# An attention and two mixing layers on one core: float16 products for a second piece, an earlier conversion, and one load for two weights

## The chip, the cores and the metric

The kernel runs on one core of one Trainium2 chip. The metric is device time in microseconds (us), the median of the runs; lower is better. The engines are PE (TensorE, the matrix products), DVE (VectorE), ACT (ScalarE) and POOL (GpSimd); SP issues the DMAs. Each engine works through its own queue in order, and semaphores hold one back until another has finished.

## The reference, cut to what matters

Three layers follow each other, all in float32 (the weights of the last two arrive as float64):

```python
# attention: q, k, v are (2, 8, 768, 64); 4 sink keys, window of 128
scores = where(is_sink | in_window, scale * q @ k.T, -1e9)
a = exp(scores - max); a = a / (sum(a) + 1e-9)
x = (a @ v)                                   # heads joined: (2, 768, 512)
# first mixing layer, 512 -> 2048 -> 512
xn = (x - mean) / sqrt(var + 1e-6) * g_ln
x = x + maximum(xn @ w_ch1, 0) @ w_ch2
# second mixing layer
theta = x @ w_theta
u = x + w_tok_r @ (x * cos(theta)) + w_tok_i @ (x * sin(theta))   # over the 768 tokens
out = u + maximum(u @ w_ch, 0)
```

## The kernel before, in words

The tokens are cut into six pieces of 256 (three for each of the two batches), each of two tiles of 128. Attention goes piece by piece and head by head. A head's scores are made by PE in a PSUM bank, DVE adds the mask and finds the maximum (L394), ACT makes the exponentials (L397), and the weights are transposed so that PE can multiply them with v. For pieces 2 to 5 the weights are split into two float16 parts and transposed by a DMA (`send_w`). For pieces 0 and 1 (`TURNED = 2`) PE transposes them in float32 (`turn_w`, L443), one copy brings them from PSUM to SBUF (ACT at even heads, L449, DVE at odd ones, L447), and the product with v is a float32 one (`values`, L477) with v as it was loaded (`whole_v`). Piece 1 also needs the sink keys: `turn_sinks` transposes their 16 columns (L457), and DVE copies them (L458). All products with v go through one PSUM bank of their own after the first piece, and DVE empties it (L494) before the next head's product.

For pieces 2 to 5 v is split into float16 parts, a high and a low one (`split_v`: ACT L196, DVE L198; the sink tile L190 and L198), from one staging buffer `vr`. There are five buffers for tiles of v, split and whole ones alike.

The first mixing layer runs in units. A unit multiplies one of 16 chunks of w_ch1 (`first`, L649 for units 0 to 7 in float32, L670 afterwards from split parts) and of w_ch2 (`second`, L696), each 128x512. Piece 0 takes units 0 to 15, piece 1 units 8 to 23, piece 2 units 16 to 31, and so on: from unit 8 on two pieces share a unit. The attention of the later pieces is interleaved with the units; the order on PE is written out by hand (`run`), with due times such as `READY1` by which a piece's attention must be done.

The weights are float64 in memory. `load_w12` loads a chunk's two matrices, one after the other, and `load64` turns each into float32: a DMA of 512 KB into one of four staging buffers, DVE L555, ACT L556 and L558, DVE L559, in that dependence. Chunks 0 to 3 are converted in the attention of piece 0 (`PRE`); afterwards unit u asks for the chunks up to u + 2 (u + 3 from unit 7 on), by `AHEAD = (2, 3)`. The ACT operations of such a conversion are placed behind the relu of unit u on ACT's queue (`behind`). The staging buffers are two x tiles that are not used yet (of pieces 4 and 5) and two of their own. The order on ACT, DVE and SP is made by a planner from its own estimates of durations; work of pieces 0 and 1 is put ahead in it (`ahead`).

Of the kernel before, what the change touches and what calls it, by code (L numbers as in the profile page):

```python
# [21 lines left out]
NT = S // 128  # L22
# [27 lines left out]
READY2 = 13.0  # L50
RATE = 7.0
PRE = [10, 15, 20, 24]
AHEAD = (2, 3)
START = 2
EARLY = 38.0

# [13 lines left out]
class Net:  # L70
# [110 lines left out]
    def split_v(self, b, t):  # L181

        if (b, t) in self.v3:
            return
        nc, p = self.nc, self.att
        r = p["vr"].tile([128, DM], F32, tag="vr", name="vr")
        nc.sync.dma_start(out=r, in_=self.vt[b, t])
        if t == NT:
            o = p["v"].tile([128, DM], F16, tag="vk", name="vk", bufs=1)
            nc.scalar.activation(o, r, AF.Copy, scale=VSC)  # L190
            r, lo, hi = r[64:96], o[64:96], o[64:96]
            self.v3[b, t] = o
# [82 lines left out]
    def attn_fast(self, eng):  # L275

        steps = [(piece, h) for piece in range(NP) for h in range(H)]
        nc, p, qk, scored, turned, sent, late = self.nc, self.att, {}, [], [], [], []

        def load(j, eng=eng):  # L280
            if j < len(steps):
                piece, h = steps[j]
                if h % 2 == 0:
                    qk[piece, h] = qk[piece, h + 1] = self.split_qk(piece, h // 2, eng)

        def load_v(piece):
            if piece < NP:
                b, tiles = self.tiles(piece)
                if piece < TURNED:
                    for t in tiles:  # L290
                        self.whole_v(b, t)
                    return
                for t in ([tiles[0] - 1] if tiles[0] else []) + tiles + ([NT] if tiles[-1] >= 2 else []):
                    self.split_v(b, t)

        def ahead(piece):
            return self.tc.high_priority() if piece < TURNED else ExitStack()

        def turn():

            piece, h, pt, st = scored.pop(0)
            b, tiles = self.tiles(piece)
            with ahead(piece):
                blocks = self.turn_w(pt, tiles, h)
            sinks = []
            if tiles[0]:
                p["ws"].append(p["ws"].pop(0))
                sinks = [p["ws"][-1][0:NSK, i] for i in range(PIECE)]
                if not turned:

                    pool, tag = self.vbanks[self.vturn % len(self.vbanks)]
                    self.vturn += 1
                    with ahead(piece):
                        self.turn_sinks(pool.tile([128, 512], F32, tag=tag, name="pv"), pt, sinks)
            turned.append((piece, h, blocks, sinks, st, pt))

        def finish(head):

            piece, h, blocks, sinks, st = head[:5]
            b, tiles = self.tiles(piece)  # L320
            with ahead(piece):
                self.values(b, h, tiles, piece, blocks, sinks, st, turned[0] if turned and turned[0][3] else None)
                if h % (H // 2) == H // 2 - 1:
                    self.stats(piece, h // (H // 2))
            if h == V_RANGE:
                while late:
                    q, ts = self.tiles(late.pop())
                    for t in ts:
                        if (q, t) in self.v3:
                            with self.behind():  # L330
                                self.range_v(q, t)
            if h == H - 1:
                with ahead(piece):
                    self.norm(piece)
                late.append(piece)

        load(0, self.nc.vector)
        load_v(0)
        for j, (piece, h) in enumerate(steps):
            b, tiles = self.tiles(piece)  # L340
            if h == 0:
                self.x[piece] = self.xp.tile([128, PIECE, DM], F32, tag=f"x{piece}", name=f"x{piece}")
            load(j + 2)
            if h == (3 if piece else V_NEXT) and piece != TURNED - 1:
                load_v(piece + 1)
            pt, st = yield from self.softmax(h, tiles, qk[piece, h])
            if piece < TURNED:
                scored.append((piece, h, pt, st))
            else:
                sent.append((piece, h) + self.send_w(pt, tiles) + (st,))  # L350
            if piece < TURNED and h == H - 1:

                while scored:
                    turn()
                    yield
                    finish(turned.pop(0))
                    yield
                while turned:
                    finish(turned.pop(0))
                if piece == TURNED - 1:  # L360
                    load_v(piece + 1)
                yield
                continue
            if len(scored) > (TURN if piece < TURNED else 0):
                turn()
                yield

            if len(turned) > (1 if scored else 0):
                finish(turned.pop(0))
            elif len(sent) > LAG:  # L370
                finish(sent.pop(0))
        while sent:
            yield
            finish(sent.pop(0))
        for t in tiles:
            self.range_v(b, t)
        self.range_whole()

    def softmax(self, h, tiles, qk):

        nc, p = self.nc, self.att
        n = len(tiles)
# [2 lines left out]
        for i, t in enumerate(tiles):  # L385
# [10 lines left out]
                op1=ALU.min, accum_out=st[:, 0, i:i + 1]),  # L396
                nc.scalar.activation(e, e, AF.Exp, bias=st[:, 0, i:i + 1], scale=-1.0,  # L397
                                     accum_out=st[:, 1, i:i + 1])]
        self.inverse(st, PSC * VSC if qk[1] is not None else 1.0)
        return pt, st  # L400

    def send_w(self, pt, tiles):
# [30 lines left out]
    def turn_w(self, pt, tiles, h):  # L433
# [7 lines left out]
        for x, (i, t) in enumerate(keys):  # L441
            c0 = (t + 1 - tiles[i]) * KW
            nc.tensor.transpose(ps[:, x * 128:(x + 1) * 128], pt[:, i, c0:c0 + 128], self.ident)  # L443
        wt = self.att["wt"].tile([128, m, 128], F32, tag="wt", name="wt")
        ps = ps[:, 0:m * 128].rearrange("p (m k) -> p m k", k=128)
        if h % 2:
            nc.vector.tensor_copy(wt, ps)  # L447
        else:
# [3 lines left out]
    def turn_sinks(self, bank, pt, sinks):  # L452
# [2 lines left out]
        ps = bank[0:NSK, 256:512].rearrange("p (i k) -> p i k", k=128)  # L455
        for i in range(PIECE):
            nc.tensor.transpose(ps[:, i], pt[:, i, 128:128 + NSK], self.ident)  # L457
        nc.vector.tensor_copy(self.att["ws"][-1][0:NSK], ps)  # L458

    def values(self, b, h, tiles, piece, blocks, sinks, st, after):  # L460

# [3 lines left out]
        pv = pool.tile([128, 512], F32, tag=tag, name="pv")  # L465
        hc = slice(h * D, (h + 1) * D)
        for i in range(len(tiles)):
            if piece < TURNED:
                prods = [(a, self.whole[b, t][:, hc]) for (j, e, t), a in blocks.items() if j == i]
                if sinks:  # L470
                    prods.append((sinks[i], self.whole[b, 0][0:NSK, hc]))
            else:
                prods = [(a, v[:, hc]) for (j, e, t), a in blocks.items() if j == i for v in self.v3[b, t][:2 - e]]
                if sinks:
                    prods.append((sinks[i], self.v3[b, NT][:, hc]))
            for j, (a, m) in enumerate(prods):
                nc.tensor.matmul(pv[:, i * D:(i + 1) * D], a, m, start=j == 0, stop=j == len(prods) - 1)  # L477
# [20 lines left out]
    def attn_general(self, eng):  # L498

        nc, p = self.nc, self.att  # L500
        for piece in range(NP):
            b, tiles = self.tiles(piece)
            self.x[piece] = self.xp.tile([128, PIECE, DM], F32, tag=f"x{piece}", name=f"x{piece}")
            if tiles[0] == 0:
                for t in range(NT):
                    self.load_v(b, t)
# [35 lines left out]
            self.norm(piece)  # L542
            yield


    def load64(self, src, stage, dst, tag):

        nc = self.nc
        n = dst.shape[-1]
        raw = stage.tile([128, n, 2], I32, tag=tag, name="raw")  # L550
        nc.sync.dma_start(out=raw.rearrange("p n w -> p (n w)"), in_=src.bitcast(I32))
        hi, flat = raw[:, :, 1], raw.rearrange("p n w -> p (n w)")
        half = flat.bitcast(U16).rearrange("p (n w) -> p n w", w=4)
        parts = dst.bitcast(U16).rearrange("p (n w) -> p n w", w=2)
# [14 lines left out]
    def load_w12(self, f):  # L569
        if f in self.w12f:  # L570
            return
        self.w12f[f] = []
        for e in range(2):
            t = self.wraw.tile([128, DM], I32, tag="w", name="w12")
            self.rawp.append(self.rawp.pop(0))
            self.load64(self.w12[f, e], self.rawp[-1][0], t, self.rawp[-1][1])
            self.w12f[f].append(t.bitcast(F32))

    def stats(self, piece, half):

# [239 lines left out]
    def run(self, general):  # L820
# [7 lines left out]
        rp = lambda name, bufs=1: pool("right", name, bufs, side="right")  # L828
        self.x, self.w12f, self.v3, self.xnorm, self.h, self.acc, self.bn, self.relu, self.whole = ({} for _ in range(9))
        self.xp = pool("all", "x")  # L830
        self.wraw = pool("left", "wraw", 2 * NF)
        self.wsp = pool("left", "wsp", 3)
        self.xT = pool("left", "xT")
        self.ln = pool("left", "ln")
# [13 lines left out]
        else:  # L848
# [3 lines left out]
            for w in a["wbuf"]:  # L852
                nc.gpsimd.memset(w[:, 0:PIECE], 0.0)
            ws = rp("a_ws")
            a["ws"] = [ws.tile([128, PIECE, 128], F32, name=f"ws{i}") for i in range(2)]
            raw = rp("a_raw")
            attn = self.attn_fast
        self.rawp = [(self.xp, f"x{NP - 2 + i}") for i in range(2)] + ([] if general else [(raw, f"r{i}") for i in range(2)])

        sb, hb, vb = (self.ps_s, "s"), (self.ps_h, "h"), (self.ps_v, "pv")  # L860
        ab = [(self.ps_a, f"a{i}") for i in range(4)]
# [237 lines left out]
```

## Time and profile before

| | |
|---|---|
| median of 3 runs | 623.66 us (617.91 to 625.28) |
| the profiled execution | 617.65 us, of which the span from first to last instruction is 615.9 us |
| mean granted TensorE clock in it | 0.983 |
| PE busy | 584.7 us, 95% |
| PE weight loads | 479.8 us, 78% |
| DVE busy | 408.5 us, 66% |
| ACT busy | 334.0 us, 54% |

The attention of piece 0 ends near 35 us, unit 0 starts at 44.6 us, the attention of piece 1 ends near 100 us, and unit 8 starts at 117.5 us. Busy shares are means over all stages; the first stages have other limits than the rest. PE's busy time is partly modelled, as its instructions overlap.

### The profile page before, as it was taken

What the parts mean: (1) busy time and instruction counts of PE and PEld (TensorE: products, weight loads), DVE (VectorE), ACT (ScalarE), POOL (GpSimd) and SP (SyncE); (2) the same over time, 40 slices, a digit from 0 to 9 for tenths busy, and PEclk for the clock granted to TensorE, in tenths of its full rate; (3) what the DMA queues carried; (4) which work ended last, traced back from release to release, by engine and by line L of the source; (5) the groups of instructions that cost most, each with busy time, mean ns of one, the idle gap of its engine ahead of it and who ended that gap; (6) DMA issues with size and microseconds to landing.
All of it is one profiled execution on the core that took longest, in us unless ns stands there. A gap on an engine that the chain in (4) does not pass through costs nothing.

```text
span 615.9 us, 9332 instructions
## 1 busy us (share of the span) xinstructions
PE 584.7 (95%) x3473; PEld 479.8 (78%) x3473; DVE 408.5 (66%) x925; ACT 334.0 (54%) x732; POOL 60.1 (10%) x53
## 2 busy tenths in 40 slices
PE   5969998899999999999999899999999899999996
PEld 3756666577777777777788678888999789999996
DVE  4763465889867776976775643367798789754262
ACT  3834563998755656655556633346676656532020
POOL 1000000000000000000021200001343332300100
PEclk9999997899999999999999989999999999999998
DMA  7641442789722533433312310000232322010112
GB/s 274 215 159 44 160 156 86 251 209 222 130 54 49 117 82 71 96 69 60 78 54 101 103 51 2 0 1 1 102 104 104 103 69 70 1 35 34 36 36 74
DMA packets 55367, 56.41 MB, mean 92 GB/s; under 512 B 40080, under 2 KB 43152, under 8 KB 55312
## 3 DMA queue, kind: packets, MB, share of 16 engines
q1 hardware_dynamic: 55312, 55.72, 32.0%
q8 instruction: 29, 0.48, 0.3%
q14 instruction: 26, 0.21, 0.1%
HBM read 43.12 MB, written 3.15 MB: 75 GB/s over the span
## 4 chain that ended last, share of the span: by engine, by line
PE 69%; DVE 13%; DMA 7%; ACT 6%; issue 2%; POOL 1%; SPq 0%; ACTq 0%; POOLq 0%
PE acc L696 19%; PE h L670 18%; PE s L273 9%; PE m L781 5%; PE f L812 5%; PE pv L477 5%; PE h L649 3%; DVE st L559 2%; DMA raw<-wtok 2%; DMA raw<-w 2%; PE th L740 2%; PE wp L443 2%; ACT st L558 1%; ACT raw L556 1%; DVE st L555 1%
## 5 line engine op out<-in xcount | busy, mean ns | idle before, releaser
L638 DVE TENSOR_TENSOR wl<-w,wh 128x512 fp32r<-128x512 f32 x96 | 69.0, 723 | 53.4 <-ACT wh L637 26.7
L637 ACT ACTIVATE wh<-w 128x512 fp32r<-128x512 f32 x96 | 59.9, 628 | 77.5 <-PE acc L696 44.0
L670 PE MATMUL h<-xT,wh 128*128 128x512 f32 (+1 forms) x384 | 96.8, 388 | 2.4 <-DVE w L555 2.4
L670 PEld LDWEIGHTS h<-xT,wh 128*128 128x128 f32 x384 | 67.1, 191 | 18.2 <-ACT xT L625 2.6
L696 PE MATMUL acc<-wh,hh 128*128 128x512 f32 x176 | 73.2, 416 | 0.0
L397 ACT ACTIVATE p<-p,st 128x272 f32<-128x272 f32 (+1 forms) x96 | 47.4, 494 | 43.7 <-DVE st L394 43.3
L696 PE MATMUL acc<-wl,hh 128*128 128x512 f32 x176 | 69.6, 395 | 0.0
L696 PE MATMUL acc<-wh,hl 128*128 128x512 f32 x176 | 69.5, 395 | 0.0
L394 DVE CUSTOM_DVE_ANT_0 p<-s,mask 128x272 f32<-128x272 f32 (+1 forms) x96 | 39.3, 411 | 29.7 <-PE s L273 28.9
L670 PE MATMUL h<-xT,wl 128*128 128x512 f32 (+1 forms) x192 | 48.8, 376 | 0.0
L696 PEld LDWEIGHTS acc<-wh,hh 128*128 128x128 f32 x176 | 33.5, 190 | 9.4 <-issue 1.2
L556 ACT ACTIVATE raw<-raw 128x512 f32<-128x512 f32 (+1 forms) x52 | 37.0, 715 | 6.5 <-DVE st L555 6.4
L670 PEld LDWEIGHTS h<-xT,wl 128*128 128x128 f32 x192 | 35.0, 191 | 6.8
L477 PE MATMUL pv<-v,wt 128*128 128x64 f16 (+1 forms) x472 | 38.2, 228 | 1.9 <-DVE x L494 1.9
L696 PEld LDWEIGHTS acc<-wh,hl 128*128 128x128 f32 x176 | 33.5, 190 | 7.8 <-DVE hl L675 0.3
L696 PEld LDWEIGHTS acc<-wl,hh 128*128 128x128 f32 x176 | 33.4, 190 | 6.0 <-DVE wl L638 0.4
L767 POOL TENSOR_TENSOR x<-xh,xl 128x512 f32<-128x512 f32 x12 | 19.3, 1607 | 131.1 <-DVE r L761 131.1
L597 POOL TENSOR_TENSOR rs<-rs,mhalf 128x2 f32<-128x2 f32 x6 | 4.8, 805 | 266.9 <-ACT rs L596 266.9
L675 DVE SCALAR_TENSOR_TENSOR hl<-h,hh 128x512 fp32r<-128x512 f32 (+1 forms) x48 | 30.7, 639 | 0.2 <-ACT hh L674 0.2
L273 PE MATMUL s<-raw 64*128 64x272 f32 (+1 forms) x64 | 24.1, 520 | 6.9 <-DMA raw<-qk 6.4
L558 ACT ACTIVATE st<-raw 128x768 uint16<-128x768 uint16 (+1 forms) x20 | 19.4, 971 | 18.6 <-DMA raw<-wtok 7.2
L674 ACT ACTIVATE hh<-h 128x512 fp32r<-128x512 f32 (+1 forms) x48 | 26.5, 552 | 5.5 <-PE h L670 5.5
(287 smaller groups left out, 1442.3 us busy)
## 6 DMA issues: line engine op xcount, KB each, us to landing
raw<-w SPq DMA_DIRECT2D x32, 512.0 KB, 4.3
raw<-wtok SPq DMA_DIRECT2D x12, 768.0 KB, 4.2
raw<-qk SPq DMA_DIRECT2D x16, 336.0 KB, 3.0
vr<-vt SPq DMA_DIRECT2D x14, 256.0 KB, 3.0
out_dram<-o SPq DMA_DIRECT2D x24, 128.0 KB, 1.7
raw<-qk SPq DMA_DIRECT2D x8, 272.0 KB, 4.0
raw<-wth SPq DMA_DIRECT2D x4, 512.0 KB, 3.3
raw<-wch SPq DMA_DIRECT2D x4, 512.0 KB, 3.3
```

Source lines behind the costliest of these rows:

```text
L273: self.nc.tensor.matmul(ps, q[:, c], k[:, k0:k0 + kn], start=j == 0, stop=j == len(prods) - 1)
L394: self.newest = [nc.vector.tensor_tensor_reduce(out=e, in0=ps[:, c0:WIN], in1=self.mask[min(t, 2)], scale=-0.125, scalar=3e38, op0=ALU.add ...
L397: nc.scalar.activation(e, e, AF.Exp, bias=st[:, 0, i:i + 1], scale=-1.0, accum_out=st[:, 1, i:i + 1])]
L477: nc.tensor.matmul(pv[:, i * D:(i + 1) * D], a, m, start=j == 0, stop=j == len(prods) - 1)
L556: nc.scalar.activation(hi.bitcast(F32), hi.bitcast(F32), AF.Copy, scale=2.0 ** -112)
L637: nc.scalar.activation(hi, r, AF.Copy)
L638: nc.vector.tensor_tensor(out=lo, in0=r, in1=hi.bitcast(F32), op=ALU.subtract)
L670: nc.tensor.matmul(ps[:, 0:n], a[:, k * 128:(k + 1) * 128], x[:, k, c], start=m == 0, stop=m == 11)
L675: nc.vector.scalar_tensor_tensor(out=hl, in0=ps[:, 0:n], scalar=0.0, in1=hh.bitcast(F32), op0=ALU.max, op1=ALU.subtract)
L696: nc.tensor.matmul(ps, a[:, c], w, start=m == 0 and n == 0, stop=m == NF - 1 and n == len(prods) - 1)
L781: nc.tensor.matmul(ps, z[i][e][:, c * 128:(c + 1) * 128], w[:, t], start=s == 0 and m == 0 and c % 2 == 0, stop=s == NT - 1 and m == 5 and ...
L812: nc.tensor.matmul(ps, self.w_last[k][e][:, c * 128:(c + 1) * 128], u[k][f], start=m == 0, stop=m == 11)
```

## The change

Piece 1 multiplies with v in float16 parts. Its weights are still transposed by PE in float32, but are brought from PSUM as two float16 parts, the high one by ACT and the low one by DVE, for every head; the sinks likewise. A block's product is high with high, high with low, and low with high. For that, piece 1's tiles of v are split like those of pieces 2 to 5, tiles 1, 2, 3 and the sink tile, and a low part `vl` of the sinks is added; only piece 0 uses whole v. `load_v(2)` now comes at head 3 of piece 1 and not at its end. `AHEAD` becomes (4, 4). A chunk's two matrices are loaded by one DMA of 1 MB and converted in one set of operations 1024 wide; the staging buffers become two of twice the size, and the x tiles of pieces 4 and 5 become one tile, `last`.

```diff
-AHEAD = (2, 3)
+AHEAD = (4, 4)
@@ split_v @@
+            if b == 0:
+                self.vl = p["v"].tile([128, DM], F16, tag="vl", name="vl", bufs=1)
+                nc.vector.scalar_tensor_tensor(out=self.vl[0:32], in0=r[0:32], scalar=VSC, in1=o[0:32], op0=ALU.mult,
+                                               op1=ALU.subtract)
@@ attn_fast @@
-                if piece < TURNED:
+                if piece == 0:
...
-                blocks = self.turn_w(pt, tiles, h)
+                blocks = self.turn_w(pt, tiles, h if piece == 0 else None)
...
-            if h == (3 if piece else V_NEXT) and piece != TURNED - 1:
+            if h == (3 if piece else V_NEXT):
                 load_v(piece + 1)
...
-                if piece == TURNED - 1:
-                    load_v(piece + 1)
@@ turn_w @@
+        if h is None:
+            wt = self.att["wt"].tile([128, 2 * m, 128], F16, tag="wt", name="wt")
+            nc.scalar.activation(wt[:, 0:m], ps, AF.Copy, scale=PSC)
+            nc.vector.scalar_tensor_tensor(out=wt[:, m:], in0=ps, scalar=PSC, in1=wt[:, 0:m], op0=ALU.mult,
+                                           op1=ALU.subtract)
+            return {(i, e, t): wt[:, e * m + x] for e in range(2) for x, (i, t) in enumerate(keys)}
@@ turn_sinks @@
-        nc.vector.tensor_copy(self.att["ws"][-1][0:NSK], ps)
+        ws = self.att["ws"][-1]
+        nc.scalar.activation(ws[0:NSK, 0], ps, AF.Copy, scale=PSC)
+        nc.vector.scalar_tensor_tensor(out=ws[0:NSK, 1], in0=ps, scalar=PSC, in1=ws[0:NSK, 0], op0=ALU.mult,
+                                       op1=ALU.subtract)
@@ values @@
+                if sinks and piece < TURNED:
+                    prods += [(sinks[i][e], v[0:NSK, hc]) for e, v in (
+                        (0, self.v3[b, NT]), (0, self.vl), (1, self.v3[b, NT]))]
@@ load_w12 @@
-        for e in range(2):
-            t = self.wraw.tile([128, DM], I32, tag="w", name="w12")
-            self.rawp.append(self.rawp.pop(0))
-            self.load64(self.w12[f, e], self.rawp[-1][0], t, self.rawp[-1][1])
-            self.w12f[f].append(t.bitcast(F32))
+        t = self.wraw.tile([128, 2 * DM], I32, tag="w", name="w12")
+        self.rawp.append(self.rawp.pop(0))
+        self.load64(self.w12[f].rearrange("e p n -> p e n"), self.rawp[-1][0], t, self.rawp[-1][1], 2)
+        t = t.bitcast(F32)
+        self.w12f[f] = [t[:, 0:DM], t[:, DM:]]
@@ run @@
-        self.rawp = [(self.xp, f"x{NP - 2 + i}") for i in range(2)] + ([] if general else [(raw, f"r{i}") for i in range(2)])
+        self.rawp = [(self.xp, "last")] + ([] if general else [(raw, "r")])
```

## Rows read from the trace of the kernel before

**Rows 1.** The head of the profile's page: the span.
```profile
span 615.9 us, 9332 instructions
```

**Rows 2.** Busy time by stretch: length, each engine's busy us, granted clock, DMA share, GB/s.
```profile
10.00:35.00 25.00, 25.00 (x95) 19.85 (x94) 17.40 (x62) 19.38 (x57) 0.00 (x0) 1.00 0.75 263
35.00:45.00 10.00, 5.04 (x16) 3.54 (x16) 7.05 (x21) 2.13 (x7) 0.71 (x1) 1.00 0.39 141
45.00:55.00 10.00, 10.00 (x34) 6.61 (x33) 1.79 (x7) 2.64 (x8) 0.00 (x0) 1.00 0.10 34
55.00:90.00 35.00, 34.28 (x173) 24.08 (x172) 19.16 (x61) 21.92 (x55) 0.00 (x0) 1.00 0.43 140
90.00:105.00 15.00, 12.99 (x46) 9.15 (x46) 7.30 (x18) 2.60 (x8) 0.83 (x1) 0.77 0.26 88
105.00:117.50 12.50, 10.14 (x46) 6.49 (x45) 11.33 (x31) 12.50 (x29) 0.00 (x0) 0.98 0.62 212
117.50:125.00 7.50, 7.48 (x20) 5.10 (x21) 6.60 (x18) 7.50 (x22) 0.00 (x0) 0.58 0.82 229
```

**Rows 3.** The chain that ended last, 55 to 131 us: start, duration, what.
```profile
55.11 1.92 PE h L649 x8
57.47 1.70 PE pv L477 x12
...
91.15 4.14 DMA raw<-w
...
96.40 3.24 PE pv L477 x12
99.64 3.71 PE h L649 x8
...
117.53 2.07 PE h L670 x4
...
120.57 3.57 PE h L670 x8
...
126.41 2.04 PE h L670 x8
128.44 0.42 PE pv L477 x14
```

**Rows 4.** Timeline of PE and ACT, 96 to 118 us: idle before, and its releaser, in brackets.
```profile
96.40 0.96 PE L477 MATMUL pv<-v,wt 128*128 128x64 f32 x4 [1.89 <-DVE x L494]
96.98 0.63 ACT L196 ACTIVATE v<-vr 128x512 f16<-128x512 f32 x1 [6.81 <-PE pv L477]
...
116.90 0.57 ACT L625 ACTIVATE xT<-tp 128x512 fp32r<-128x512 f32 x1
117.52 2.07 PE L670 MATMUL h<-xT,wh 128*128 128x512 f32 x4 [2.39 <-DVE w L555]
```

**Rows 5.** Groups by shape, 44.6 to 117.5 us: busy, mean ns; idle before.
```profile
L558 ACT ACTIVATE w<-raw 128x512 uint16<-128x512 uint16 x14 | 10.8, 770 | 0.0
L559 DVE SCALAR_TENSOR_TENSOR w<-raw,w 128x512 int32<-128x512 int32 x13 | 8.8, 680 | 2.4 <-ACT w L558 2.4
L556 ACT ACTIVATE raw<-raw 128x512 f32<-128x512 f32 x13 | 8.5, 655 | 0.0
L555 DVE TENSOR_SCALAR w<-raw 128x512 uint16<-128x512 uint16 x12 | 5.5, 457 | 9.0 <-DMA raw<-w 9.0
L458 DVE COPY ws<-pv 16x256 f32<-16x256 f32 x8 | 3.3, 410 | 6.9 <-PE pv L457 6.8
L447 DVE COPY wt<-wp 128x512 f32<-128x512 f32 x4 | 2.7, 679 | 0.9 <-PE wp L443 0.8
L449 ACT ACTIVATE wt<-wp 128x512 f32<-128x512 f32 x4 | 2.4, 588 | 2.1 <-PE wp L443 2.1
L198 DVE SCALAR_TENSOR_TENSOR v<-vr,v 128x512 f16<-128x512 f32 x2 | 1.4, 688 | 1.4 <-ACT v L196 1.4
L657 ACT ACTIVATE xT<-x 128x1024 fp32r<-128x1024 f32 x1 | 1.0, 1029 | 0.0
```

More of the change, by code (lines that the diff above doesn't have):

```diff
@@ L307, in turn @@
                 p["ws"].append(p["ws"].pop(0))
-                sinks = [p["ws"][-1][0:NSK, i] for i in range(PIECE)]
+                sinks = [[p["ws"][-1][0:NSK, e, i] for e in range(2)] for i in range(PIECE)]
                 if not turned:
@@ L341, in attn_fast @@
             if h == 0:
-                self.x[piece] = self.xp.tile([128, PIECE, DM], F32, tag=f"x{piece}", name=f"x{piece}")
+                self.x[piece] = self.new_x(piece)
             load(j + 2)
-            if h == (3 if piece else V_NEXT) and piece != TURNED - 1:
+            if h == (3 if piece else V_NEXT):
                 load_v(piece + 1)
-            pt, st = yield from self.softmax(h, tiles, qk[piece, h])
+            pt, st = yield from self.softmax(b, h, tiles, qk[piece, h])
             if piece < TURNED:
@@ L377, in attn_fast, with softmax @@
         self.range_whole()
-    def softmax(self, h, tiles, qk):
+    def softmax(self, b, h, tiles, qk):
         nc, p = self.nc, self.att
@@ L398, in softmax @@
                                      accum_out=st[:, 1, i:i + 1])]
-        self.inverse(st, PSC * VSC if qk[1] is not None else 1.0)
+        self.inverse(st, PSC * VSC if tiles[0] or b else 1.0)
         return pt, st
@@ L443, in turn_w @@
             nc.tensor.transpose(ps[:, x * 128:(x + 1) * 128], pt[:, i, c0:c0 + 128], self.ident)
+        ps = ps[:, 0:m * 128].rearrange("p (m k) -> p m k", k=128)
+        if h is None:
[4 more added lines that the diff above has]
+            return {(i, e, t): wt[:, e * m + x] for e in range(2) for x, (i, t) in enumerate(keys)}
         wt = self.att["wt"].tile([128, m, 128], F32, tag="wt", name="wt")
-        ps = ps[:, 0:m * 128].rearrange("p (m k) -> p m k", k=128)
         if h % 2:
@@ L467, in values @@
         for i in range(len(tiles)):
-            if piece < TURNED:
+            if piece == 0:
                 prods = [(a, self.whole[b, t][:, hc]) for (j, e, t), a in blocks.items() if j == i]
-                if sinks:
-                    prods.append((sinks[i], self.whole[b, 0][0:NSK, hc]))
             else:
                 prods = [(a, v[:, hc]) for (j, e, t), a in blocks.items() if j == i for v in self.v3[b, t][:2 - e]]
-                if sinks:
+                if sinks and piece < TURNED:
+                    prods += [(sinks[i][e], v[0:NSK, hc]) for e, v in (
+                        (0, self.v3[b, NT]), (0, self.vl), (1, self.v3[b, NT]))]
+                elif sinks:
                     prods.append((sinks[i], self.v3[b, NT][:, hc]))
@@ L502, in attn_general @@
             b, tiles = self.tiles(piece)
-            self.x[piece] = self.xp.tile([128, PIECE, DM], F32, tag=f"x{piece}", name=f"x{piece}")
+            self.x[piece] = self.new_x(piece)
             if tiles[0] == 0:
@@ L543, in attn_general, with new_x, load64 @@
             yield
-    def load64(self, src, stage, dst, tag):
+    def new_x(self, piece):
+        if piece < NP - 2:
+            return self.xp.tile([128, PIECE, DM], F32, tag=f"x{piece}", name=f"x{piece}")
+        if piece == NP - 2:
+            self.last = self.xp.tile([128, 2, PIECE, DM], F32, tag="last", name="last")
+        return self.last[:, piece - NP + 2]
+    def load64(self, src, stage, dst, tag, parts=1):
         nc = self.nc
@@ L550, in load64 @@
         raw = stage.tile([128, n, 2], I32, tag=tag, name="raw")
-        nc.sync.dma_start(out=raw.rearrange("p n w -> p (n w)"), in_=src.bitcast(I32))
+        flat = raw.rearrange("p n w -> p (n w)")
+        nc.sync.dma_start(out=flat if parts == 1 else flat.rearrange("p (e n) -> p e n", e=parts), in_=src.bitcast(I32))
         hi, flat = raw[:, :, 1], raw.rearrange("p n w -> p (n w)")
@@ L571, in load_w12 @@
             return
-        self.w12f[f] = []
-        for e in range(2):
-            t = self.wraw.tile([128, DM], I32, tag="w", name="w12")
-            self.rawp.append(self.rawp.pop(0))
-            self.load64(self.w12[f, e], self.rawp[-1][0], t, self.rawp[-1][1])
-            self.w12f[f].append(t.bitcast(F32))
+        t = self.wraw.tile([128, 2 * DM], I32, tag="w", name="w12")
[3 more added lines that the diff above has]
+        self.w12f[f] = [t[:, 0:DM], t[:, DM:]]
     def stats(self, piece, half):
@@ L830, in run @@
         self.xp = pool("all", "x")
-        self.wraw = pool("left", "wraw", 2 * NF)
+        self.wraw = pool("left", "wraw", NF)
         self.wsp = pool("left", "wsp", 3)
@@ L854, in run @@
             ws = rp("a_ws")
-            a["ws"] = [ws.tile([128, PIECE, 128], F32, name=f"ws{i}") for i in range(2)]
+            a["ws"] = [ws.tile([128, 2, PIECE, 128], F16, name=f"ws{i}") for i in range(2)]
             raw = rp("a_raw")
             attn = self.attn_fast
-        self.rawp = [(self.xp, f"x{NP - 2 + i}") for i in range(2)] + ([] if general else [(raw, f"r{i}") for i in range(2)])
+        self.rawp = [(self.xp, "last")] + ([] if general else [(raw, "r")])
         sb, hb, vb = (self.ps_s, "s"), (self.ps_h, "h"), (self.ps_v, "pv")
```

## The prediction

> **What bounds the kernel now.** The profiled execution took 617.65 us for a span of 615.9 us [rows 1]; the median of the three runs is 623.66 us, 6.0 us above it. I make the sum against 617.65 and subtract it from the median; that these 6 us stay is a choice.
>
> I read the stretches first, because the change acts only before some 160 us. In the view by stretch [rows 2] the reader is to see four states. From 10 to 35 us PE is busy throughout, with ACT 19.38 and DVE 17.40 of 25 us. From 35 to 45 us PE has half its time idle, in the norm of piece 0. From 45 to 90 us PE is all but full, while DVE and ACT are at about half. Then 90 to 125 us is bad: idle PE, a granted clock of 0.77 and later 0.58, ACT nearly empty until 105 us and full after it.
>
> The chain of waits [rows 3] says what fills PE there: a head's product with v is 12 matmuls in 1.70 us, about as long as a unit's whole first product (1.92). It also shows a weight DMA (4.14 us, landing at 95.29) standing ahead of a product. The timeline [rows 4] shows the two stalls. At 96.40 PE has waited 1.89 us for DVE's L494, and ACT stood 6.81 us at L196: the split of a tile of v found no free buffer until a product of piece 1 had read its whole tile. At 117.52 PE has waited 2.39 us before unit 8. The row names L555, but ACT's L625, one of this product's inputs, ended at 117.47: ACT's backlog is as good a releaser.
>
> **The product in float16.** A head has four blocks and two sink products, so 6 x 3 = 18 float16 matmuls replace its 12. Fourteen such matmuls of piece 2 take 0.42 us [rows 3], 0.030 each, so 18 take 0.54. That saves 1.70 - 0.54 = 1.16 us a head, and 8 x 1.16 = 9.3 us of PE.
>
> The price lies on the other two engines [rows 5]. Instead of one copy by either engine, ACT now makes a high part for each head and DVE a low part: ACT 4 more at 0.588, 2.4 us; DVE 4 more at 0.679, 2.7 us. For the sinks ACT gets 8 operations; no row shows that shape on ACT, so between 0.2 (below the DVE copy) and 0.588 each, and I take the DVE copy's 0.410, 3.3 us. DVE's subtraction replaces its copy at about the same price. The path from transposes to product becomes ACT then DVE. Its cover is the head between; if that is gone, the next thing late is the single PSUM bank, which L494 and both sink parts have to release.
>
> Does the PE gain survive? From 45 to 117.5 us DVE is busy 1.79 + 19.16 + 7.30 + 11.33 = 39.6 us and waits 9.0 us for weight DMAs [rows 2, 5]. Add 2.7 and one more chunk converted in this stretch, 2 x (0.457 + 0.680) = 2.3, and DVE needs 53.6 us, its waits included. PE would need 72.5 - 9.3 = 63.2, and some 56 if the stalls below went too. ACT comes to 39.7 + 2.4 + 3.3 + a chunk's 2 x (0.770 + 0.655) = 2.9, in all 48.3, less what wide operations save. So DVE becomes almost as long as PE. In-order queues don't run that full: the bounds are 0 and 9.3 us, and I take 6.3, nearer the upper end because PE still has the longer list.
>
> **The wider conversion.** One operation 1024 wide for two of 512: L657 is 1024 wide at 1.029 us, against 2 x 0.63 for L196 [rows 4, 5], 0.23 saved, by two operations and some seven chunks 3 us of ACT. That work is beside PE, so I count 0. The new cost is that DVE's first step waits for the whole 1 MB, and the next chunk's DMA on SP until all of a chunk is converted, with the q and k loads behind it in SP's queue. The pair of loads in the bad stretch landed 4.14 us after its release [rows 3], so one load of the same bytes should not be worse by more than another 4.14. I keep half of the 9.0 us of DVE waits, as the count halves.
>
> The Trainium skill ("DMA: Bandwidth & Descriptors", "Anatomy of one DMA") gives a fixed part of about 2.0 us and bytes over 436 GB/s, an estimate of 4.4 us for 1 MB. By it the waits would be no longer than now, and the sum some 1 us better; no row here shows a load of 1 MB.
>
> **Four units ahead.** Unit 0 now asks for chunk 4 and unit 1 for chunk 5, when ACT has 7.4 of 10 us free and DVE 8.2 from 45 to 55 us [rows 2]. Chunk 8, whose lateness shows at 117.52, is asked for by unit 4 and no longer by unit 6. Unit 7 asks for one chunk, no longer for two. So ACT's full stretch starts with less queued. What goes: 2.39 us of idle, and the low clock behind it, 2.07 - 1.02 and 3.57 - 2.04 (the full-clock row has 2.04 for eight) [rows 3, 4], 2.6 us; together 5.0. Norm and transposes of piece 1 remain before unit 8, so I take 4.2; bounds 0 and 5.0.
>
> **Splits of v.** Tiles 1, 2 and the sinks are split earlier, tile 4 and 5 find buffers that piece 0 has freed, and ACT's 6.81 us go. With them may go the first stall: 1.89 us of idle and the low clock behind it, 3.24 - 1.70 and 3.71 - 1.92, 3.3 us, of which 1.5 are in the product itself: 5.2 in all. But DVE's wait for a weight DMA was there too and may fall elsewhere; bounds 0 and 5.2, and I take half, 2.6. In return three splits and the low sinks fall mostly into 10 to 35 us: ACT 3 x 0.63 = 1.9 us and DVE 4 x 0.688 = 2.8 us, against 5.6 and 7.6 us free [rows 2]. One staging buffer serves them, so ACT can stand behind a landing, ahead of an exponential; piece 0 then ends later. Bounds -0.5 (two L555 of 0.457 among the norm's operations become one) and 3; I take 1.5. On SP two whole-tile loads go and three staged ones come, and the range check later loads one tile, not three: all beside other work, 0. The shared x tile costs 0, since the last chunk is asked for by unit 11 and piece 4 joins at unit 32.
>
> **Sum.** -6.3 - 4.2 - 2.6 + 1.5 = -11.6: 606.0 us for a profiled execution, 612 us beside the median. Nothing later changes except by starting earlier. Two per cent of 623.66 is 12.5 us, about what a measurement here can tell from no change, so the forecast lies just on the near side of that line.
>
> **Rivals.**
>
> *All of it* (chance 0.25). PE stays the only bound: 9.3 + 5.0 + (5.2 - the 1.5 counted in the product's own change at most) = 18 to 19.5 us; 604 to 606. For it: ACT's empty stretch from 90 to 105 us [rows 2] is filled. Against: DVE's 53.6 us of need.
>
> *Eaten by DVE and ACT* (0.22). Each head waits for the low part behind a weight DMA on DVE; or the lead is only nominal, because two staging buffers hold two chunks and the planner puts L555 right at a landing as before. Then the product brings 0 to 2, the stalls 2 to 4, and piece 0 costs 1.5: 0.5 to 4.5 us gained, 619 to 623.
>
> *PE's clock* (0.08), the slower side. The clock fell after the idle stretches before 96.40 and 117.52, and rows at the low level took 1.9 times as long (3.71 against 1.92) [rows 3]. If the shorter products leave PE waiting in each head from 45 to 105 us, the remaining 46 us or so of PE work run partly at 1.2 GHz. Each us of it costs 0.9; the 11.6 are gone after 13 us, and after 27 us it is slower by over 2%. With half of the 46 us low it is 21 - 11.6 = 9 us slower, 633; with all, 653. Against: from 35 to 45 us PE idled 5 us and the granted clock stayed at 1.00 [rows 2].
>
> The Trainium skill ("TensorE: Matmul & The Clock Gate", Part 1) makes the half rate the default that activity must lift, and so speaks against a change that thins PE's work. By that rule, this last rival would be the forecast wherever DVE leaves gaps; the trace agrees at 96 and 117 us and not at 35 to 45.
>
> **The numbers.** My own case has 0.45; its own range is 608 to 616, around 612, half a chance on either side of the 2% line at 611.2 shifted towards no change. Faster by over 2%: 0.25 + 0.19 = 0.44. Slower by over 2%: 0.06 of the clock case. Within: 0.50. The range for 8 in 10 reaches from 602, which takes in the whole gain, to 622, which takes in most of the eaten one.
>
> **What would show it.** Product: rows of 18 float16 matmuls near 0.54 us a head, and head to head some 0.8 us shorter; if that stays away, DVE or ACT bounds, and the idle before L477 will name which. Stalls: no ACT wait at L196, ACT busy in 45 to 55 us and spread in 90 to 125, granted clock 1.00 there, under 0.5 us of wait before unit 8. Waits for weight DMAs: half as many, under 5 us in all. Price: unit 0 starts at 46 us, against 44.6. I would be wrong if piece 0 ended over 3 us later, if a slice before 110 us showed a granted clock under 0.9, or if PE gained time before 120 us and lost it again by 160.

## The result, and the profile after

| | before | after |
|---|---|---|
| median | 624.27 us (617.91 to 625.28, 4 runs) | 613.65 us (612.30 to 616.41, 4 runs) |
| ratio | | 0.9896, interval [0.9853, 0.9939] |
| profiled execution | 617.65 us, clock 0.983 | 614.24 us, clock 0.985 |

The change makes the kernel 1.0% faster by the ratio, 6.5 us, and by 3.8 to 9.2 us over its interval; the two medians of four runs lie 10.6 us apart. The same kernel run again later gave 0.9881, 7.4 us (further down). The two profiled executions lie only 3.4 us apart, because the one of before is among its fastest: 6.6 us under this median, while that of after is 0.6 us above its own. A comparison of the two traces therefore shows only part of what the runs show.

Busy time by stretch, after; columns as in [rows 2] (length, then PE, PE's weight loads, DVE, ACT and POOL, granted clock, DMA share, GB/s):

```profile
35.00:45.00 10.00, 5.73 (x20) 4.52 (x20) 8.13 (x21) 3.46 (x11) 1.27 (x1) 1.00 0.70 257
45.00:55.00 10.00, 9.12 (x33) 6.71 (x32) 2.95 (x6) 4.96 (x8) 0.00 (x0) 1.00 0.07 26
...
90.00:105.00 15.00, 10.29 (x64) 6.47 (x65) 8.94 (x20) 6.96 (x15) 0.00 (x0) 0.69 0.30 104
105.00:117.50 12.50, 12.07 (x49) 7.17 (x48) 9.13 (x22) 11.38 (x26) 0.90 (x1) 0.96 0.42 127
117.50:125.00 7.50, 6.80 (x30) 4.63 (x30) 6.74 (x21) 6.65 (x17) 0.00 (x0) 1.00 1.19 222
```

Against [rows 2]: the granted clock of 117.5 to 125 us rose from 0.58 to 1.00, but that of 90 to 105 us fell from 0.77 to 0.69, and PE is busy 10.29 us there, no longer 12.99. One bad stretch is repaired, and PE stands idle longer in another. The deeper fall of the clock does not belong to the kernel: a second execution of it (the run with no edit among the experiments) has the same 10.29 us of PE there, but the clock of before, 0.77:

```profile
90.00:105.00 15.00, 10.29 (x57) 6.34 (x57) 9.44 (x20) 6.60 (x16) 0.00 (x0) 0.77 0.33 112
```

ACT works 4.96 us from 45 to 55 us, not 2.64: the lead does start the conversions there.

The chain of after through the bad stretch, and below it the timeline of the same place (idle before and its releaser in brackets):

```profile
85.58 3.62 PE h L671 x8
...
89.23 0.38 ACT hh L673
89.61 1.02 ACT raw L578
90.64 0.50 ACT p L400 x2
91.14 1.24 ACT w L580
...
92.41 0.97 DVE w L581
...
95.41 3.41 PE acc L718 x4
98.82 1.02 PE pv L490 x18
```

```profile
83.15 0.35 PE L490 MATMUL pv<-v,wt 128*128 128x64 f16 x6 [0.76 <-DVE x L507]
...
85.52 3.68 PE L671 MATMUL h<-x,w 128*128 128x256 f32 x8
...
89.23 0.38 ACT L673 ACTIVATE hh<-h 128x256 f32<-128x256 f32 x1 [4.35 <-PE h L671]
89.47 0.34 PE L490 MATMUL pv<-v,wt 128*128 128x64 f16 x6
89.51 1.13 ACT L578 ACTIVATE raw<-raw 128x1024 f32<-128x1024 f32 x1
...
90.39 0.39 PE L466 MATMUL pv<-ident,p 128*16 128x128 f32 x2
...
92.41 1.23 DVE L581 SCALAR_TENSOR_TENSOR w<-raw,w 128x1024 int32<-128x1024 int32 x1 [4.14 <-ACT w L580]
...
92.74 0.57 ACT L450 ACTIVATE wt<-wp 128x512 f16<-128x512 f32 x1
...
93.55 0.68 DVE L451 SCALAR_TENSOR_TENSOR wt<-wp,wt 128x512 f16<-128x512 f32 x1
...
94.29 1.12 PE L446 MATMUL wp<-ident,p 128*128 128x128 f32 x4 [3.51 <-DVE wt L451]
```

This is one row of work across three engines. ACT stands idle 4.35 us, because the next conversion is placed behind a unit's relu (L673), and the relu waits for PE's product. Then relu, L578, two exponentials and L580 follow each other on ACT, and behind them the high part of a head's weights (L450): it starts at 92.74, though PE's transposes for it ended at 89.63. DVE's L581 waits 4.14 us for L580; the low part of the same weights (L451) stands behind L581 in DVE's queue and starts 0.24 us after the high part has ended; and PE waits 3.51 us for the PSUM bank that this low part has to read. So most of the delay is on ACT, where the high part stands behind the conversion.

PE's unit product before it (3.68 us, 1.99 elsewhere) and the products behind the wait run at the lower clock level. In the second execution of the kernel that unit product ran at full clock, and the wait is the same, so the low clock before it does not make it:

```profile
86.48 1.99 PE L671 MATMUL h<-x,w 128*128 128x256 f32 x8
...
93.57 0.66 PE L446 MATMUL wp<-ident,p 128*128 128x128 f32 x4 [3.51 <-DVE wt L451]
```

A head's product itself is short: 89.47 to the next instruction at 90.39 is 0.92 us, for 18 matmuls.

Groups by shape, 44 to 120 us of after, against [rows 5]:

```profile
L581 DVE SCALAR_TENSOR_TENSOR w<-raw,w 128x1024 int32<-128x1024 int32 x8 | 9.8, 1224 | 12.0 <-ACT w L580 11.3 <-ACT st L501 0.6
...
L577 DVE TENSOR_SCALAR w<-raw 128x1024 uint16<-128x1024 uint16 x8 | 6.0, 746 | 4.3 <-DMA raw<-w 4.3
...
L446 PE MATMUL wp<-ident,p 128*128 128x128 f32 x32 | 5.6, 301 | 4.7 <-DVE wt L451 4.7
...
L468 ACT ACTIVATE ws<-pv 16x256 f16<-16x256 f32 x8 | 2.9, 361 | 5.8 <-PE pv L466 5.8
```

DVE's waits for weight DMAs halved (9.0 to 4.3 us), but its waits for ACT within a conversion rose from 2.4 to 11.3 us, and PE's for the low part are new.

### The profile page after: what moved, and what is told of

Read it like the earlier page. It is cut to its first block, busy times and chain, and to the rows that moved or that the text cites. A ratio compares the mean times of both kernels' runs of the same rounds, so it can differ in the third digit from the quotient of the medians.

```text
span 612.5 us, 9364 instructions
## 1 busy us (share of the span) xinstructions
PE 578.7 (94%) x3521; PEld 472.3 (77%) x3521; DVE 409.8 (67%) x898; ACT 337.3 (55%) x714; POOL 60.8 (10%) x53
## 4 chain that ended last, share of the span: by engine, by line
PE 60%; DVE 16%; ACT 10%; DMA 9%; issue 3%; POOL 1%; SPq 0%; ACTq 0%; DVEq 0%; POOLq 0%
PE acc L718 18%; PE h L692 17%; PE s L278 6%; PE m L803 5%; PE f L834 5%; PE pv L490 3%; DMA vr<-vt 3%; DMA raw<-w 2%; ACT raw L578 2%; DVE st L581 2%; PE h L671 2%; DMA raw<-wtok 2%; PE th L762 2%; ACT st L580 1%; ACT w L580 1%
## 5 line engine op out<-in xcount | busy, mean ns | idle before, releaser
L692 PE MATMUL h<-xT,wh 128*128 128x512 f32 (+1 forms) x384 | 95.1, 382 | 0.0
L578 ACT ACTIVATE raw<-raw 128x1024 f32<-128x1024 f32 (+2 forms) x36 | 34.3, 952 | 6.7 <-DVE st L577 6.4
L490 PE MATMUL pv<-v,wt 128*128 128x64 f16 (+1 forms) x504 | 33.5, 215 | 2.8 <-DVE x L507 2.0
L580 ACT ACTIVATE st<-raw 128x768 uint16<-128x768 uint16 (+1 forms) x20 | 19.5, 973 | 18.0 <-DMA raw<-wtok 6.8
L581 DVE SCALAR_TENSOR_TENSOR w<-raw,w 128x1024 int32<-128x1024 int32 x16 | 19.6, 1223 | 13.7 <-ACT w L580 12.2
```

The lines of the kernel that those rows point to most:

```text
L578: nc.scalar.activation(hi.bitcast(F32), hi.bitcast(F32), AF.Copy, scale=2.0 ** -112)
L580: nc.scalar.activation(parts[:, :, 0], half[:, :, 1], AF.Copy, scale=2.0 ** -13, bias=2.0 ** -14 - 0.5)
L581: nc.vector.scalar_tensor_tensor(out=dst, in0=hi, scalar=3, in1=dst, op0=ALU.logical_shift_left, op1=ALU.bitwise_or)
L692: nc.tensor.matmul(ps[:, 0:n], a[:, k * 128:(k + 1) * 128], x[:, k, c], start=m == 0, stop=m == 11)
```

## The experiments

Every ratio is to the kernel before on the same chip. "Unit 0" and "unit 8" are the starts of those units' first product in the profile.

**One part at a time.** The float16 product alone takes the parts of the diff in `split_v`, `attn_fast`, `turn_w`, `turn_sinks` and `values`:

```diff
-                if piece < TURNED:
+                if piece == 0:
...
-                blocks = self.turn_w(pt, tiles, h)
+                blocks = self.turn_w(pt, tiles, h if piece == 0 else None)
```

> The kernel before with the float16 product alone (its splits of v included; lead of two or three units, two loads a chunk). Theory P (the product's PE time carries the gain): 5 to 9 us faster than before, a head's 18 products near 0.54 us, and the second stall before unit 8 (2.4 us) still there. Theory L (the gain is the lead's, which removes waits and the low clock behind them): within 3 us of before, because DVE and ACT take back what PE saves, and piece 0 ends 2 to 3 us later for the splits of v.

Measured: 619.78 us, 0.9963 [0.9932, 0.9994]. PE gained, but a new wait of 4.63 us for the low part stood at 91.38 us, and another of 3.21 us at 124.39.

The lead alone:

```diff
-AHEAD = (2, 3)
+AHEAD = (4, 4)
```

> The kernel before with a lead of four units alone. Theory P: at most 3 us faster, as the first stall (the split of v waiting for a buffer) stays. Theory L: 6 to 10 us faster, no wait before unit 8 and full granted clock from 117 to 125 us.

Measured: 612.16 us, 0.9851 [0.9799, 0.9903]: the smallest edit brings more than the whole change. In its timeline unit 8 waits 0.96 us and the rows behind it are at full clock; ACT still waits 6.05 us at L196, yet PE's stall at L477 is down to 0.79 us:

```profile
97.22 1.08 PE L477 MATMUL pv<-v,wt 128*128 128x64 f32 x4 [0.79 <-DVE x L494]
...
116.88 1.17 PE L670 MATMUL h<-xT,wh 128*128 128x512 f32 x4 [0.96 <-DVE xT L626]
118.55 1.20 PE L670 MATMUL h<-xT,wh 128*128 128x512 f32 x4
```

One load and one set of operations alone (`load_w12`, the staging buffers, the shared x tile):

```diff
-            self.load64(self.w12[f, e], self.rawp[-1][0], t, self.rawp[-1][1])
+        self.load64(self.w12[f].rearrange("e p n -> p e n"), self.rawp[-1][0], t, self.rawp[-1][1], 2)
```

> The kernel before with one load and one set of operations for a chunk's two matrices alone. Both theories: between 2 us faster (less ACT and DVE time) and 4 us slower (DVE's first step waits for the whole megabyte; the waits of L555's counterpart for the weight DMA fall from 9.0 us to between 4 and 6 us in 45 to 117 us).

Measured: 617.26 us, 0.9931 [0.9883, 0.9980]. Costed at nothing, it is worth 4.3 us by itself. It works on the same place as the lead: in its trace PE's stall at L477 is 0.79 us, that before unit 8 is 0.83 us, and the clock from 117.5 to 125 us is 1.00.

The changed kernel again, beside these three, with no edit:

> The changed kernel itself, as the anchor of this set: ratio 0.985 to 0.994 against before, on the same chip as the three parts. If the parts add, its gain is the sum of the other three within 3 us; if not, one part opens room for another.

Measured: 615.49 us, 0.9881 [0.9844, 0.9918]. The parts alone sum to 0.37 + 1.49 + 0.69 = 2.55%; together they bring 1.0 to 1.2%. The gap of 1.3 points is wider than the interval of any one part (0.6 to 1.0 points). The profile of this run is the second execution of the changed kernel that is read above and below.

**Two parts.** The changed kernel with the float32 product back (lead and one load remain; the diff above reversed):

> The changed kernel without the float16 product and its splits (lead of four units and one load a chunk stay). Theory L (the lead carries the gain, the product adds nothing at the end): ratio to before 0.983 to 0.988, no slower than the whole change, unit 0 back near 44.6 us. Theory R (the product brings its 9.3 us of PE on top, and the single profile only shows it badly): 4 us or more slower than the whole change, ratio 0.993 or above.

Measured: 616.81 us, 0.9926 [0.9896, 0.9957]: above the range of theory L and just short of that of theory R. The lead thus adds nothing measurable to one load (0.9931), where alone it brought 1.5%. The lead and the one load repair the same place and replace each other; together they lose some of the lead's own gain. In the profile, an execution 3.0 us above this median, PE stops again at 136.52 us for 2.14 us, and the product after it takes 2.07 us at the low clock.

The changed kernel with two loads and two sets of operations per chunk (float16 and lead remain; the third diff reversed):

> Float16 product and lead of four units, but two loads and two sets of operations a chunk. Theory L: between the lead alone and the whole change, ratio 0.985 to 0.990; if the wide set is what delays DVE's last step (it waited 11.3 us for ACT in 45 to 120 us), this kernel is 1 to 3 us faster than the whole change; if the wide set saves work that matters, 1 to 3 us slower.

Measured: 613.44 us, 0.9875 [0.9827, 0.9923], no different from the changed kernel. The wait for the low part is 4.15 us here: the width of the conversion does not make it.

**The price at piece 0.** In after, ACT waits 4.45 us at 40.70 us for a landing of `vr`. Here the loads and splits of v, those of the third piece among them, are placed behind the newest exponential on ACT's queue:

```diff
-                load_v(piece + 1)
+                with self.behind():
+                    load_v(piece + 1)
```

> The changed kernel with the splits of v placed behind the newest exponential on ACT's queue, so that piece 2's tile 4 no longer stands in the norm of piece 0 (ACT waited 4.45 us there for its load). If that wait is what moved unit 0 from 44.6 to 47.2 us: unit 0 at 45 us or before, and 2 us faster than the whole change. If something else did (chunk conversions in the norm): unit 0 stays at 47 us and the time is the same.

Measured: 617.52 us, 0.9934 [0.9903, 0.9965]. Unit 0 starts at 44.2 us and no longer at 47.2, so this wait was the price at unit 0; but the time is not better: unit 8 comes early, at 115.1 us, and then PE stalls for 1.68 us at 132.93 us, with a clock of 0.58 from 133 to 137 us. The 2 us that the expectation gave to this wait did not come.

**PE's work in the stretch.** Each of piece 1's products is computed three times over (54 matmuls a head; each pass starts its sum anew):

```diff
+            for r in range(3 if piece == 1 else 1):
                 for j, (a, m) in enumerate(prods):
```

> The changed kernel with every product of piece 1 computed three times (54 float16 matmuls a head and not 18; the first two results are overwritten), 8 x 1.08 = 8.6 us more of PE. If PE's time in the product is what sets the pace of piece 1: 6 to 9 us slower than the whole change. If PE waits there for conversions and low parts from ACT and DVE anyway: 0 to 3 us slower. If the low clock of 85 to 105 us comes from PE having too little to do, it stays away and the time may even fall.

Measured: 627.58 us, 1.0093 [1.0056, 1.0130], some 12 to 13 us over the changed kernel. Its row from unit 0 to unit 8:

```profile
46.20:131.10 84.90, 81.43 (x633) 54.39 (x634) 44.40 (x110) 47.70 (x103) 0.69 (x1) 0.90 0.37 126
```

That is beyond the 6 to 9 us expected, which went by 0.030 us a matmul. PE's busy time is 17.66 us more than in the changed kernel (63.77 us). A head's 54 matmuls take 2.80 us up to PE's next instruction (59.46 to 62.26 us), where 18 take 0.93 in the changed kernel (59.92 to 60.85), both at full clock: 0.052 us for each added one, 15.0 us for all 288. The rest of the 17.66 goes with a lower clock later, 0.77 from 105 to 117.5 us against 0.96. Of the 17.66 us, 13.0 arrive at unit 8. PE's work is on the path: it does not merely wait for others here.

**The order on ACT.** The changed kernel, where a unit's conversion is no longer placed behind its relu:

```diff
-                self.newest = [self.relu[u]]
-                with self.behind():
-                    self.load_w12(f)
+                self.load_w12(f)
```

> The changed kernel with a chunk's conversion no longer placed behind the relu of its unit on ACT's queue. In the changed kernel PE stood 3.51 us at 94.29 for a low part; before that ACT held a relu that waited 4.35 us for its product, then the conversion, with exponentials and high parts queued behind. Theory W (the waits that ate the product's gain go through that place in ACT's queue): the stall near 90 us falls under 1.5 us and the time by 2 to 5 us. Rival (ACT and DVE are simply full from 45 to 105 us): the waits move elsewhere, idle PE of 5 us or more in 47 to 118 us remains, and the time is within 2 us of the whole change.

Measured: **609.58 us, 0.9806 [0.9742, 0.9871]**, the lowest of all. Its interval still meets that of the changed kernel at the edge. The same place in its timeline:

```profile
85.94 1.16 ACT L578 ACTIVATE raw<-raw 128x1024 f32<-128x1024 f32 x1 [0.41 <-DVE w L577]
...
87.72 0.38 ACT L673 ACTIVATE hh<-h 128x256 f32<-128x256 f32 x1 [0.63 <-PE h L671]
...
88.51 0.59 ACT L450 ACTIVATE wt<-wp 128x512 f16<-128x512 f32 x1
...
89.12 0.69 DVE L451 SCALAR_TENSOR_TENSOR wt<-wp,wt 128x512 f16<-128x512 f32 x1 [0.21 <-ACT wt L450]
...
89.87 0.66 PE L446 MATMUL wp<-ident,p 128*128 128x128 f32 x4 [0.60 <-DVE wt L451]
```

L578 runs while PE still computes the unit's product, ahead of the relu; the high part (L450) no longer stands behind a whole conversion, the low part follows it at once, and PE waits 0.60 us instead of 3.51. From 90 to 105 us the granted clock is 0.89, where the two profiles of the changed kernel have 0.69 and 0.77.

The same edit on the kernel with two loads per chunk:

> The same with two loads and two sets a chunk (float16 product, lead of four units, no place behind the relu). Theory W: faster than the same kernel behind the relu (613.4 us there) by 2 us or more, and the best of all so far, below the lead alone. Rival: within 2 us of it, with the idle PE of 7.2 us in 45 to 115 us spread to other places.

Measured: 614.56 us, 0.9879 [0.9841, 0.9918]: no gain over 0.9875, against theory W. PE's longest wait for a low part did fall, from 4.15 to 1.71 us, but unit 0 starts at 49.2 us and no longer at 45.4, and unit 8 at 116.7 us and no longer at 114.7; between them PE still loses 5.8 of 67.5 us. So taking the wait away is by itself no gain, and why the edit pays with the wide conversion and not here stays open.

The kernel before, run as an experiment:

> The kernel before once more, for the profile of another of its executions: its first profile had a granted clock of 0.983 at 617.65 us, its runs have 0.965 to 0.985 at 618 to 625 us. If the spread is the granted clock, this one's mean clock and time fall on the same line, about 0.4 us for each 0.001, and the profile shows in which stretch the clock is low; if it is not, stretches of equal clock differ in length.

Measured: 622.69 us, 1.0016 [0.9983, 1.0049]. Its profile has a span of 622.2 us at a clock of 0.970, a usual run of this kernel, unlike the first one. Over its ten runs the time falls from 626.0 to 618.0 us as the mean clock rises from 0.968 to 0.983, about 0.5 us for each 0.001, close to the line of the expectation. Its timeline where unit 8 starts:

```profile
118.25 1.20 PE L670 MATMUL h<-xT,wh 128*128 128x512 f32 x4 [2.47 <-ACT xT L625]
...
121.69 2.08 PE L670 MATMUL h<-xT,wh 128*128 128x512 f32 x4 [1.69 <-DVE xT L626]
123.57 1.91 PE L670 MATMUL h<-xT,wl 128*128 128x512 f32 x4
...
126.38 2.07 PE L670 MATMUL h<-xT,wh 128*128 128x512 f32 x4
...
129.36 2.07 PE L670 MATMUL h<-xT,wh 128*128 128x512 f32 x4
131.23 1.91 PE L670 MATMUL h<-xT,wl 128*128 128x512 f32 x4
```

Two stalls, 2.47 and 1.69 us, and five groups at the low clock up to 133 us; the full-clock groups take 1.20 and 1.07.

**What the product gives once the order is right.** The last run takes the float32 product back in the fastest kernel:

> The changed kernel with two edits: the second piece's product with v back in float32 (12 matmuls of 1.70 us a head), and the conversion that a unit asks for no longer placed behind that unit's relu. Theory: the float16 product's shorter time was hidden behind relu, conversion and low part in one row on ACT and DVE, and with that placing gone the 8 heads give 7 to 9 us; then this kernel, which lacks the float16 product, stands 6 to 9 us above the 609.58 us of the changed kernel without the placing: 615.5 to 618.5, a ratio of 0.990 to 0.995 to the kernel before, and from unit 0 to unit 8 it needs 69 to 72 us where that one needed 62. Rival: dropping the placing is worth some 4 to 7 us whatever the product's type, and the float16 product still only 1 to 3; then this kernel takes 610.5 to 613, a ratio of 0.982 to 0.986, and unit 0 to unit 8 takes 64 to 67 us.

Measured: 613.07 us, 0.9861 [0.9810, 0.9911]. That is the rival's side of the expectation, by a little: the product is worth 0.55%, some 3.4 us, and not 7 to 9; the two intervals overlap, so the runs alone do not separate the two kernels. The other half of the rival holds as well: without the float16 product, dropping the placing takes the ratio from 0.9926 to 0.9861, 4.0 us, and with it from 0.9881 to 0.9806, 4.7 us. The placing thus costs about the same whatever the product's type, and the runs do not show that it held back the product's gain in particular. The rows from unit 0 to unit 8 say where the rest goes. The kernel without the float16 product and the one with it, both with the free order:

```profile
48.00:115.10 67.10, 66.28 (x298) 45.53 (x298) 47.79 (x114) 47.18 (x99) 0.83 (x1) 0.97 0.56 188
```

```profile
49.40:111.60 62.20, 59.12 (x345) 38.02 (x345) 49.55 (x118) 51.33 (x111) 0.86 (x1) 0.97 0.61 202
```

And the same pair with the conversion behind the relu, without and with the float16 product (the second is the changed kernel; a third row is its second execution):

```profile
45.70:118.20 72.50, 70.30 (x297) 47.65 (x297) 42.18 (x106) 43.18 (x91) 0.83 (x1) 0.93 0.43 147
```

```profile
47.20:118.10 70.90, 63.77 (x346) 40.77 (x346) 43.48 (x110) 45.85 (x102) 0.90 (x1) 0.90 0.43 150
```

```profile
47.34:116.70 69.36, 62.28 (x346) 39.55 (x346) 43.41 (x110) 45.90 (x102) 0.79 (x1) 0.95 0.45 153
```

| the float16 product, in profiles | PE busy | PE not busy | unit 0 starts | unit 8 starts |
|---|---|---|---|---|
| free order | -7.16 | +2.26 | +1.4 | -3.5 us |
| behind the relu | -6.53 | +4.93 | +1.5 | -0.1 us |
| behind the relu, second execution | -8.02 | +4.88 | +1.6 | -1.5 us |

PE saves some 7 us either way. Behind the relu, waits take back 4.9 of it and the later unit 0 another 1.5, so that 0.1 us is left at unit 8 in one execution and 1.5 in the other. In the free order half of it arrives. These are single executions, and that of the kernel without the product behind the relu is 3.0 us above its median; the medians above show less of a difference between the two orders.

**What comes later.** The chains near 350 us of before, after and the fastest kernel, in this order; all three wait there for the conversion of a matrix of the second layer:

```profile
355.26 0.66 PE tp L615 x4
355.92 5.71 PE acc L696 x18
```

```profile
353.69 0.66 PE tp L637 x4
354.35 4.12 PE acc L718 x18
```

```profile
347.38 1.11 PE tp L637 x4
348.49 6.46 PE acc L718 x18
```

At the transposes the fastest kernel is 6.3 us ahead of after, and behind the same 18 matmuls only 3.5 (354.95 against 358.47). After was 1.6 us ahead of before and becomes 3.2. The 18 matmuls take 4.12 us where the granted clock of 345 to 365 us is 1.00, 5.71 at 0.91 and 6.46 at 0.83. So part of a lead is lost or found here by the clock alone. It is not the change: in the second profiles of before and of the changed kernel the same 18 matmuls take 6.52 and 5.71 us, so two executions of one kernel differ as much. No experiment was made on that place.

## Why the prediction was right, and where it was not

The forecast was 612 us; the median is 613.65. The total was right, most of its terms were not, and their errors cancelled: that is luck. Part of it lies in the medians, too. I took 11.6 us off 623.66, and the gain is 6.5 us by the ratio and 7.4 when the kernel was run again, with upper ends of 9.2 and 9.7 us; 11.6 is above both.

- **Product, -6.3.** Two steps were mis-sized. A head's 18 matmuls take 0.92 us up to the next instruction and not 0.54, since 0.030 us of piece 2's matmuls was taken as the price here. Measured the same way in before, the 12 of float32 take 1.80 us and the 14 of piece 2 take 0.51 (rows below), so the PE gain is 8 x (1.80 - 0.92) = 7.0 us, not 9.3 (the profiles: 6.5 to 8.0). And "its cover is the head between" failed: the cover was gone where the high part stood behind a conversion on ACT, 3.51 us of wait at 94.29. DVE's waits for ACT within a conversion, 2.4 us before and 11.3 after, were no term of the sum. Of the PE gain, 0.1 and 1.5 us are left at unit 8 in the two profiles; by the ratios the product is worth 1.9 to 2.8 us in the changed kernel (0.9926 against 0.9896 and 0.9881).

```profile
57.30 0.56 PE L477 MATMUL pv<-v,wt 128*128 128x64 f32 x4
...
59.10 0.39 PE L457 MATMUL pv<-ident,p 128*16 128x128 f32 x2
...
128.29 0.35 PE L477 MATMUL pv<-v,wt 128*128 128x64 f16 x6
...
128.80 0.39 PE L273 MATMUL s<-hi 64*128 64x272 f32 x1
```

- **Lead, -4.2, bounds 0 to 5.** Alone it brought 9.3 us (6.0 to 12.5), beyond the bound. I read its price from a profile that was one of the kernel's best. In the usual profile of before, the stalls are 2.47 + 1.69 us and the five slow groups take 10.04 us where 1.20 and 1.07 each would make 5.74, 4.3 us more: 8.5 us, nearly all of which the lead removes. Together with one load it brought 0.3 us (0.9931 to 0.9926), on the float16 product with two loads 5.5 us (0.9963 to 0.9875).
- **Wide conversion, 0.** Alone worth 4.3 us; beside the lead alone it costs 4.7 (0.9851 to 0.9926, on two chips and with intervals that touch), beside lead and product about nothing.
- **Splits of v, -2.6.** ACT's wait at L196 went from 6.81 us to 1.13 at its successor, as said, but it was not what stopped PE: with the lead alone it stayed, 6.05 us, and PE's stall fell to 0.79 all the same. In after, PE still waits 1.20 us at 101.35 for the same bank. This step of the argument is wrong.
- **Piece 0, +1.5.** Unit 0 starts at 47.2 us, 2.6 later, within the bounds; the wait on `vr` was the mechanism I had named, and taking it away moved unit 0 back to 44.2.
- **"Nothing later changes".** Not refuted. Of the 3.4 us between the two spans 1.6 arise near 350 us, but by a clock that differs between executions of one kernel.

Of the signs that I had named, these came: no wait ahead of unit 8 (118.06 us), ACT's work at 45 to 55 us, weight DMA waits under 5 us, full clock from 117.5 us. These failed: 0.54 us a head (0.92), no wait of ACT for the split of v (1.13 us), unit 0 at 46 us (47.2), and the clock: it is 0.69 from 90 to 105 us, and I had said that a slice before 110 us under 0.9 would show me wrong. That sign says little, since before has 0.77 there. It is PE's 4.9 us of new waits that show the rival *Eaten by DVE and ACT* to be the truth about the product, while the lead paid for it. The third rival, the clock, happened from 85.5 us to some 105 in one profile of the changed kernel and from about 94 us in the other; unit 8 starts at 118.1 and 116.7 us in them, against 117.5 and 118.3 in the two of before.

The Trainium skill ("DMA: Bandwidth & Descriptors", "Anatomy of one DMA") gave an estimate of 4.4 us for a load of 1 MB, from a fit that the section makes for loads issued by GpSimd. The loads here are issued by SP: the 16 of the changed kernel landed in a median of 5.4 us, 1.0 us above the estimate, and the halves of 512 KB took 4.3 us before. The Trainium skill has the lower clock as the default that activity lifts ("TensorE: Matmul & The Clock Gate", Part 1). From 90 to 105 us the traces bear this out only in part: PE's busy time fell from 12.99 to 10.29 us in both profiles of the changed kernel, and the granted clock went from 0.77 to 0.69 in one of them and stayed at 0.77 in the other.

## What to carry to other kernels

When a product becomes shorter but its operand now passes through two engines in a row, look in the trace at what else stands in those two queues ahead of either operation: here PE saved some 7 us and met 4.9 us of new waits, the longest behind a weight conversion tied to a relu. Do not take it that removing such a wait returns the gain: untying the conversion was worth 4 to 5 us with either product, and nothing with two loads a chunk, though the wait was gone there too. Two edits that repair the same stall do not add, so time each alone before summing them. And price a stall from a usual run: the profile of a fast one showed 5.0 us where the usual one has 8.5. For the same reason, read a low clock in a second execution before you call it the kernel's.

## What the runs showed of the hardware that was not expected

- A float16 matmul of 64 columns in this order (six with 128 rows of weights, then three with 16, twice) costs 0.051 us on PE, 0.92 for 18 up to the next instruction, where 14 of another piece, all with 128 rows of weights, took 0.51, 0.036 each. That the order is the reason was not tested.
- The granted clock fell in one execution with hardly a wait ahead of it, and not in another of the same kernel. In after, PE was busy 5.00 of 5 us from 75 to 80 us and waited 0.76 us at 83.15, and the product at 85.52 took 3.68 us, not 1.99; in the second execution PE waited 0.87 us at 84.11, and the same product, at 86.48, took 1.99.
- Computing each product three times over (17.66 us more of PE) left the stretch's granted clock at 0.90; the two profiles of the changed kernel have 0.90 and 0.95.
